# Column means of 512 of w1's columns taken later, and PSUM tiles from two halves in turn

## The chip, the cores and the metric

One core of one Trainium2 chip runs the kernel. The metric is the device time of an execution in microseconds. Engines work side by side, each through its own queue in order: TensorE (PE, with its weight loads as PEld), VectorE (DVE), ScalarE (ACT), GpSimd (POOL), and SyncE (SP), which issues DMAs.

## The reference

An input x (2048 tokens of 512 channels) goes through two layers. The first normalizes x per token, multiplies it by y, and adds x; y is a causal convolution over the 2048 tokens, per channel, of kv with ssm_k, where kv is v times a four-tap shift of k. The second normalizes the sum h per token and applies a two-layer perceptron with ReLU.

```python
x = A_q
h = x + A(layernorm(x), A_k, A_v, A_shift_k, A_ssm_k, A_ssm_D)
h2 = h + relu(layernorm(h) @ B_w1) @ B_w2        # w1 is 512 x 1376, w2 is 1376 x 512
# inside A(q, k, v, ...):
kv = (sum over t of k shifted by t, times shift_k[:, t]) * v
y  = irfft(rfft(kv, 4096) * rfft(ssm_k, 4096))[:2048] + kv * ssm_D
return q * y
```

The layernorm has no learned weights. The mean of h over the channels is taken off in w1: the mean of each column of w1 is subtracted from the column once, and h goes into the product as it is; 1/std is multiplied in at the end.

## The kernel before

The convolution is a Fourier transform written as matrix products. Forward stages (`to_rows`, `taps`, `stage1`) put the filter's half-done transform into the SBUF tile BK and that of kv into BX. The **product loop** (L501 to L517) finishes both transforms and multiplies them: 8 chunks c of 4 frequencies, in each four units of kind u (`pairs`, u0 to u3) and two of kind s (`sums`, s0 and s1; tile us). A unit has one PSUM tile: TensorE's steps K fill one half of it from BK, steps X the other from BX. Then `times` runs: ScalarE copies the K half to SBUF (L442), and VectorE multiplies the X half by it into BK or BX (L494); this product is the tile's last reader. A step of a u unit is 4 matmuls; an s unit has four such steps (K1, X1, K2, X2). The order of all steps is a string: FIRST for chunk 0, OTHER for chunks 1 to 7. A unit's tile is allocated at its first step, and in the code's order released at its "=".

Then two **inverse stages**. `inv1` (L612, tile psi) has 16 blocks b of 4 groups. A group has a matmul of 256 columns from BXs (the s units' results) and two of 128 from BK (the u units' results). The matmuls from BXs of blocks 0 and 1 run ahead (`inv1_begin`). ScalarE or VectorE copies a block into the tile ax. `inv2(q)` (L686, tile pz) makes a quarter q of the tokens from ax, and `gate(q)` (L679) multiplies it by the normalized x and adds x. Quarters 0 and 1 come first, into two PSUM tiles, psZ0 and psZ; then the perceptron (`mlp1`, `mlp2`) and the other two quarters take turns. `inv2(0)` stands between `inv1` and the gate of quarter 0.

**PSUM.** Until the end of inv1 every PSUM tile comes from `bank2` (L151): 2 x 512 fp32 numbers per partition, from a pool psF (L93) of four such slots, which is all of PSUM. When psF is closed (L731), psZ and psZ0 (L732, L733) are put in its place, psZ in the first half of PSUM and psZ0 in the second.

**The column means.** `wsum` (1376 fp32 numbers per partition) is w1 added over its four blocks of 128 rows, made by GpSimd in the product loop (`add_chunks`). After the loop `column_means` (L522) multiplies it by a matrix of 1/512 to get each column's mean on all partitions: four matmuls of FS = 344 columns into two tiles pm. The second tile is copied to SBUF by ScalarE (L626). `center(n)` (L587) subtracts the means from w1 on VectorE; all four are issued after block 0 of inv1, followed by `ec_wrap(1)` and the statistics of x's first quarter. The perceptron is the first to read w1. After inv1 two matmuls of zeros (`fill`, L647, tile psz) run on TensorE.

The order of all work is written out by hand (`manual_schedule`): each engine takes its instructions in the order of the code.

Of the kernel before, what the change touches and what calls it, by code (L numbers as in the profile page):

```python
# [9 lines left out]
ALU = mybir.AluOpType  # L10
BF16 = mybir.dt.bfloat16
F32 = mybir.dt.float32
F32R = mybir.dt.float32r
I32 = mybir.dt.int32
PSUM = bass.MemoryType.PSUM
P = 128
# [40 lines left out]
def kernel(  # L57
# [13 lines left out]
    nc = tc.nc  # L71
    _, S, D = A_q.shape
    DFF = B_w1.shape[1]
# [3 lines left out]
    DC = D // P  # L77
# [5 lines left out]
    pl = _Pools(tc)  # L83
# [6 lines left out]
    turnp = pl.push("turnp")  # L90
    early = pl.push("early", side="right")
    kp = pl.push("kp", side="right")
    psum = pl.push("psF", bufs=4, space=PSUM)  # L93

# [52 lines left out]
                             bias=(pbias if neg else nbias)[:])  # L149

    def bank2(name):  # L151
        return psum.tile([P, 2, 512], F32, tag="ps", name=name)[:]

    def fill(ps, n):

        for _ in range(n):
            nc.tensor.matmul(out=ps, lhsT=zero[:], rhs=zero[:].unsqueeze(1).to_broadcast([P, 4, P]), start=True, stop=True, skip_group_check=True)  # L157

    fill(bank2("psz")[:, 0, :], 7)

    n1i = early.tile([P, 1], I32, name="n1i")
# [15 lines left out]
    for t in (identw, ident):  # L177
        nc.gpsimd.memset(t[:], 0.0)
        nc.gpsimd.affine_select(out=t[:], in_=t[:], compare_op=ALU.not_equal, fill=1.0,
                                base=0, pattern=[[-1, P]], channel_multiplier=1)  # L180
    psw = bank2("psw")[:, 0, 0:KS * DC].rearrange("p (j r) -> p j r", j=KS)
    for j in range(KS):
        nc.tensor.matmul(out=psw[:, j, :], lhsT=wrow[:, j::KS], rhs=ident[0:DC, 0:DC], start=True, stop=True, skip_group_check=True)
    fill(bank2("psz")[:, 0, :], 17)
    nc.gpsimd.iota(r2, pattern=[[2, 32], [128, 64]], base=1, channel_multiplier=0)
    pi4 = consts.tile([P, 2], I32, name="pi4")
# [73 lines left out]
    def ec_turns(q):  # L260
        w = ecw[q]
        nc.gpsimd.iota(w[:, 1, :].rearrange("p (i a n) -> p i a n", i=4, a=4), pattern=[[1, 4], [16, 4], [64, 32]],
                       base=4 * q, channel_multiplier=0)
        for h, off in ((0, 4096 + 2048), (1, 0)):
            nc.gpsimd.tensor_scalar(out=w[:, h, :], in0=w[:, 1, :], scalar1=k1o[:], scalar2=float(off),
                                    op0=ALU.mult, op1=ALU.add)

    def ec_wrap(q):
        nc.vector.tensor_single_scalar(out=ecw[q], in_=ecw[q], scalar=8191, op=ALU.bitwise_and)

    def ec_sins(q, rs=range(DC)):
        for r in rs:
            nc.scalar.activation(out=ecore[q][:, :, :, r // 2, r % 2, :], in_=ecw[q].rearrange("p h (i x) -> p h i x", i=4),
                                 func=ACT.Sin, scale=esc[:, r:r + 1], bias=ebi[:, r:r + 1])
# [73 lines left out]
    ones = consts.tile([P, P], F32R, name="ones")  # L348
# [66 lines left out]
    BXt = bxp.tile([P, 32, 66, DC * 2], F32R, tag="X", name="BX")  # L415
# [14 lines left out]
    wsum = stf[:, 0:DFF]  # L430
# [85 lines left out]
        if c in (2, 4, 5):  # L516
            add_chunks(max(c - 3, 0))  # L517

    FS = 344
    cen = {}  # L520

    def column_means(ns):  # L522
        ps = bank2("pm")
        for b, n in enumerate(ns):
            cen[n] = ps[:, b, 0:FS]
            nc.tensor.matmul(out=cen[n], lhsT=ones[:], rhs=wsum[:, n * FS:(n + 1) * FS], start=True, stop=True)
        return ps[:, :, 0:FS]

    column_means((0, 1))
    pm23 = column_means((2, 3))  # L530
    pl.pop("skp")
    pl.pop("stp")
    pl.pop("prod")
# [5 lines left out]
    def load_x(q):  # L539
        for a, src in enumerate(_tokens(x_d, 4 * q, 4)):  # L540
            nc.sync.dma_start(out=xh[q][32 * a:32 * a + 32].rearrange("p t d -> p (t d)"), in_=src)
# [14 lines left out]
    qT = [late.tile([P, 4, DC, P], BF16, name="qT0")[:]] + [None] * 3  # L556
# [15 lines left out]
    def lift(q):  # L572
        rows_T(xT[q], xh[q])

    def ln1_stats(q):
        stats(xh[q], mv1, rstd1, q)

    def ln1_norm(q, src=None):

        src = xh[q] if src is None else src  # L580
        for i in range(4):
            t = 4 * q + i
            nc.vector.tensor_scalar(out=src[:, i, :], in0=src[:, i, :], scalar1=mv1[:, t, 0:1],
                                    scalar2=rstd1[:, t, :], op0=ALU.subtract, op1=ALU.mult)
        rows_T(qT[q], src)

    def center(n):  # L587
        fs = slice(n * FS, (n + 1) * FS)
        nc.vector.tensor_tensor(out=w1[:, :, fs], in0=w1[:, :, fs],
                                in1=cen[n].unsqueeze(1).to_broadcast([P, DC, FS]), op=ALU.subtract)  # L590

    ax1 = late.tile([P, 32, 2, P], F32R, name="ax1")
    ax = (BX[:, 1].rearrange("p n k x -> p n (k x)").rearrange("p n (m c) -> p n m c", m=2), ax1[:])
# [12 lines left out]
    def inv1_begin(b):  # L606

        blocks[b] = bank2("psi").rearrange("p b (i d a n) -> p (b i) d a n", i=2, d=2, a=2)
        for i in range(4):
            inv1_mm(b, i, (0,), sums_first=True)  # L610

    def inv1(b, eng):  # L612
        n = 4 // len(eng)
        for i0, e in zip(range(0, 4, n), eng):
            begun = b in blocks and not i0
            if not begun:
                blocks[b] = bank2("psi").rearrange("p b (i d a n) -> p (b i) d a n", i=2, d=2, a=2)
            for i in range(n):
                inv1_mm(b, i, (1, 2) if begun else (0, 1, 2), i0)
            for rho in range(2):  # L620
                copy(e, ax[rho][:, :, :, 8 * b + 2 * i0:8 * b + 2 * i0 + 2 * n],
                     blocks[b][:, 0:n].rearrange("p i d a n -> p a n (i d)")[:, rho].rearrange("p (n m) c -> p n m c", m=2))

    lift(0)
    later = qT[0].rearrange("p i r t -> p (i r t)").bitcast(F32)[:, 0:2 * FS].rearrange("p (n f) -> p n f", n=2)
    nc.scalar.copy(out=later, in_=pm23)  # L626
    cen[2], cen[3] = later[:, 0], later[:, 1]
    inv1_begin(0)
    inv1_begin(1)

# [3 lines left out]
    for b in range(16):  # L634
        inv1(b, "ADAD" if b == 15 else "AD" if b == 14 else "D" if b in (7, 9, 11, 13) else "A")
        if b == 0:
            for n in range(4):
                center(n)
            ec_wrap(1)
            ln1_stats(0)  # L640
        if b == 3:
            ln1_norm(0)
        if b in (8, 9, 10, 11):
            ec_sins(1, (b - 8,))
        if b == 11:
            load_x(1)
    fill(bank2("psz")[:, 0, :], 2)  # L647
    M = bkp.tile([P, 32768], BF16, tag="K", name="M")
    top = [0]

# [25 lines left out]
    def flat(t):  # L676
        return t.rearrange("p i r t -> p (i r t)")

    def gate(q):  # L679
        nc.vector.tensor_tensor(out=flat(qT[q]), in0=pzs[q][:].rearrange("p i r a n -> p (i r a n)"), in1=flat(qT[q]), op=ALU.mult)  # L680
        nc.vector.tensor_tensor(out=flat(xT[q]), in0=flat(qT[q]), in1=flat(xT[q]), op=ALU.add)
        hT[q] = xT[q]
        nc.sync.dma_start_transpose(out=xh[q].rearrange("p i (r c) -> p (i r) c", r=DC),
                                    in_=hT[q].rearrange("p i r t -> p (i r) t"))

    def inv2(q, pool):  # L686
        pz = pool.tile([P, 4, DC, 4, 32], F32, tag="pz", name="pz")
        pzs[q] = pz
        for j in range(16):
            i, a = j // 4, j % 4  # L690
            w = min(2, 4 - a)
            n2 = 16 * a + 4 * q + i
            for rho in range(2):
                nc.tensor.matmul(out=pz[:, i, :, a:a + w, :].rearrange("p (s r) a n -> p s r (a n)", s=2),  # L694
                                 lhsT=ax[rho][:, n2 // 2, n2 % 2, :],
                                 rhs=ecore[q][:, rho, i, :, :, 32 * a:32 * a + 32 * w],
                                 start=(rho == 0), stop=(rho == 1), skip_group_check=True)
# [30 lines left out]
            if hook is not None:  # L728
                hook(i)

    pl.pop("psF")  # L731
    psz = pl.push("psZ", space=PSUM)  # L732
    psz0 = pl.push("psZ0", space=PSUM)  # L733
    ec_turns(2)
    inv2(0, psz0)
    gate(0)
    inv2(1, psz)
    pl.pop("psZ0")
# [68 lines left out]
```

## Time and profile before

| | us |
|---|---|
| median of 3 runs | 206.26 (206.26 to 206.31) |
| profiled execution | 206.31 |
| its span, first to last instruction | 204.2 |
| TensorE busy | 195.3 (96%) |
| VectorE busy | 141.0 (69%) |
| ScalarE busy | 114.7 (56%) |
| GpSimd busy | 79.6 (39%) |

The difference of 2.1 us between the execution and its span lies around the span. The mean granted TensorE clock is 0.994 of full speed. In the timeline a row gives the start and the length in us of a group of like instructions, the engine, the line, the operation, the tiles it writes and reads (out<-in), the shape, the count, and in brackets the engine's idle time before it and what ended that. Ends of matmuls are modelled, so starts are compared.

Where the stages stand in the span: product loop 48.6 to 83.6, column means 83.6 to 84.7, inv1 84.7 to 107.9, inv2 of two quarters 108.5 to 116.2, the perceptron and the rest 116.2 to 204.2.

### The profile page before, as it was taken

The numbers are of one execution on the slowest core, as the hardware profiler recorded it, in microseconds if no ns is written. First come the engines' busy times: TensorE is split into PE (matmuls) and PEld (weight loads), VectorE is DVE, ScalarE is ACT, GpSimd is POOL, SyncE is SP. The second block draws the span as 40 slices with busy tenths as digits, with TensorE's granted clock in tenths as the row PEclk, the third lists the DMA queues.
The fourth block names the chain that finished last, engine by engine and source line by source line (L and its number), as shares of the span: only waits on it lengthen the run. The fifth ranks groups of instructions, "written<-read, shape, count | busy, mean of one in ns | idle before, by whom it ended". The sixth has DMA issues, their size and how long they took to land.

```text
span 204.2 us, 4733 instructions
## 1 busy us (share of the span) xinstructions
PE 195.3 (96%) x1929; PEld 137.2 (67%) x1929; DVE 141.0 (69%) x246; ACT 114.7 (56%) x188; POOL 79.6 (39%) x127
## 2 busy tenths in 40 slices
PE   8899999898999999999999999999999999999991
PEld 2475556887899999899998844475445844444460
DVE  4999888698799998997561967995378660360131
ACT  4987875788578877686880088205940164026300
POOL 7969999960559995212003032062002200002000
PEclk9999999999999999999999999999999999999997
DMA  6999990002600000052636999997643605110011
GB/s 178 337 178 207 176 176 3 3 5 31 248 3 0 3 3 0 22 132 55 106 87 184 207 215 196 171 174 91 91 82 76 135 19 103 32 58 17 0 51 51
DMA packets 47300, 19.94 MB, mean 98 GB/s; under 512 B 42186, under 2 KB 45744, under 8 KB 47280
## 3 DMA queue, kind: packets, MB, share of 16 engines
q1 hardware_dynamic: 43616, 16.14, 41.7%
q10 hardware_dynamic: 3664, 3.51, 6.0%
q8 instruction: 15, 0.25, 0.5%
q14 instruction: 5, 0.04, 0.1%
HBM read 7.02 MB, written 2.10 MB: 45 GB/s over the span
## 4 chain that ended last, share of the span: by engine, by line
PE 88%; DVE 7%; ACT 2%; issue 1%; DVEq 0%
PE ps1m L706 19%; PE ps2m L722 19%; PE psi L603 11%; PE us L478 9%; PE pz L694 7%; PE u L456 7%; PE ps L308 7%; PE pkv L340 5%; PE psz L157 2%; PE pst L291 1%; DVE E L343 1%; DVE BK L320 1%; DVE G L227 1%; DVE E L44 1%; DVE G L225 1%
## 5 line engine op out<-in xcount | busy, mean ns | idle before, releaser
L708 ACT ACTIVATE M<-ps1m 128x512 bf16<-128x512 f32 (+1 forms) x44 | 25.1, 595 | 49.4 <-PE ps1m L706 39.0
L722 PE MATMUL ps2m<-M 128*128 128x512 bf16 (+3 forms) x187 | 38.7, 366 | 0.0
L722 PEld LDWEIGHTS <-M 128*128 128x128 bf16 (+1 forms) x187 | 18.3, 98 | 19.9
L706 PEld LDWEIGHTS <-w 128*128 128x128 bf16 (+1 forms) x176 | 17.4, 100 | 19.9
L565 POOL TENSOR_SCALAR rstd<-mv 128x4 f32<-128x4 f32 x8 | 2.2, 277 | 70.1 <-DVE mv L563 70.1
L402 POOL TENSOR_TENSOR smc<-st 64x256 fp32r<-64x256 f32 x32 | 22.8, 732 | 12.4 <-PE us L478 11.5
L724 DVE SCALAR_TENSOR_TENSOR M<-ps2m,rstd,M 128x512 bf16<-128x512 f32 (+1 forms) x13 | 9.2, 707 | 24.8 <-PE ps2m L722 16.3
L494 DVE TENSOR_TENSOR BK<-u,ktu 128x512 fp32r<-128x512 f32 x32 | 21.2, 685 | 3.5 <-ACT ktu L442 1.9
L603 PE MATMUL psi<-inv,BK 128*128 128x128 f32 x128 | 21.1, 255 | 0.0
L442 ACT COPY ktu<-u 128x512 f32<-128x512 f32 x32 | 18.0, 592 | 5.2 <-PE u L456 4.2
L603 PE MATMUL psi<-inv,BX 128*128 128x256 f32 x64 | 20.5, 337 | 0.0
L603 PEld LDWEIGHTS psi<-inv,BK 128*128 128x128 f32 x128 | 19.7, 197 | 0.0
L706 PE MATMUL ps1m<-M,w 128*128 128x512 bf16 (+1 forms) x88 | 19.3, 379 | 0.0
L706 PE MATMUL ps1m<-xT,w 128*128 128x512 bf16 (+1 forms) x88 | 19.3, 379 | 0.0
L478 PE MATMUL us<-BK,smc 64*128 64x256 f32 x128 | 14.5, 302 | 0.6 <-ACT BX L278 0.6
L456 PE MATMUL u<-BK,st 64*128 64x256 f32 x128 | 13.6, 290 | 0.2 <-DVE BX L494 0.2
L478 PE MATMUL us<-BX,smc 64*128 64x256 f32 x128 | 13.3, 282 | 0.0
L323 ACT CAST BK<-ps 128x512 fp32r<-128x512 f32 x16 | 9.4, 586 | 6.6 <-PE ps L308 4.9
L456 PE MATMUL u<-BX,st 64*128 64x256 f32 x128 | 13.0, 281 | 0.0
L603 PEld LDWEIGHTS psi<-inv,BX 128*128 128x128 f32 x64 | 12.1, 196 | 0.3 <-DVE BK L494 0.3
L561 DVE BATCH_NORM_STATS2 st<-M 128x6 f32<-128x512 bf16 x20 | 12.3, 676 | 0.0
L494 DVE TENSOR_TENSOR BX<-us,kts 128x512 fp32r<-128x512 f32 x16 | 11.0, 686 | 0.8 <-ACT kts L442 0.5
(132 smaller groups left out, 407.2 us busy)
## 6 DMA issues: line engine op xcount, KB each, us to landing
E<-in_A_ssm_k_dram SPq DMA_DIRECT2D x1, 2048.0 KB
out_dram<-M ACTq DMA_DIRECT2D x15, 128.0 KB
w<-in_B_w_dram SPq DMA_DIRECT2D x1, 1376.0 KB
M<-in_B_w_dram ACTq DMA_DIRECT2D x1, 1280.0 KB
M<-in_A_q_dram SPq DMA_DIRECT2D x8, 128.0 KB
xh<-in_A_q_dram SPq DMA_DIRECT2D x4, 128.0 KB
xr<-in_A_q_dram SPq DMA_DIRECT2D x4, 128.0 KB
out_dram<-M ACTq DMA_DIRECT2D x2, 64.0 KB
```

The source lines that it names most:

```text
L308: nc.tensor.matmul(out=pss[rp][:, gi // 2, :, gi % 2, :], lhsT=fl[rows, 2 * g:2 * g + 2, :].rearrange("p d n -> p (d n)"), rhs=f[rows].rea ...
L402: nc.gpsimd.tensor_tensor(out=smc[pq, c % 3, i, :, 64 * dp:64 * dp + 64], in0=st[pq, ks, 64:128].bitcast(F32), in1=st[pq, ks, 0:64].bitcas ...
L442: nc.scalar.copy(out=kt[:], in_=ps)
L456: nc.tensor.matmul(out=ps[:, dp, 256 * x:256 * x + 256], lhsT=t[pq], rhs=cols((BK, BX)[x], pq, k1, i), start=not begun, stop=(i == 1), til ...
L478: mm = nc.tensor.matmul(out=ps[:, k % 2, 256 * x:256 * x + 256], lhsT=smc[pq, k // 4 % 3, i, k % 4, :], rhs=cols((BK, BX)[x], pq, k, i), s ...
L494: nc.vector.tensor_tensor(out=o, in0=ps[:, :, 256:512].rearrange("p b (g x) -> p b g x", x=8), in1=kt[:].rearrange("p b (g x) -> p b g x", ...
L561: nc.vector.bn_stats(out=st[:, i, :], in_=src[:, i, :])
L603: nc.tensor.matmul(out=o if part == 0 else o[:, P * part - P:P * part], lhsT=src[:, g // 2, :, g % 2::2].rearrange("p c r -> p (c r)"), rh ...
L694: nc.tensor.matmul(out=pz[:, i, :, a:a + w, :].rearrange("p (s r) a n -> p s r (a n)", s=2), lhsT=ax[rho][:, n2 // 2, n2 % 2, :], rhs=ecor ...
L706: nc.tensor.matmul(out=ps1[:fsz, :].rearrange("p (i t) -> p i t", i=4), lhsT=w1[:, c, fc * P:fc * P + fsz], rhs=hT[sc][:, :, c, :], start= ...
L708: nc.scalar.activation(out=h1T[:fsz, fc, :], in_=ps1[:fsz, :], func=ACT.Relu)
L722: nc.tensor.matmul(out=ps2, lhsT=h1T[:ksz, fc, i * P:(i + 1) * P], rhs=w2[:ksz, fc, d0:d0 + w], start=(fc == 0), stop=(fc == NFC - 1))
```

## The change

The pool of four slots becomes two pools of two slots, psFa and psFb; `bank2` takes from them in turn. The columns of w1 are cut into 512, 352 and 512. The means of the first two parts are taken where all were before, into one tile. The sums of the last part are copied by ScalarE to an unused piece of the tile BX (`wlast`); their means are taken after inv1, in place of one of the two matmuls of zeros, in a tile of the first half. The copy of the second pm tile to SBUF is gone. The first two parts are centered after block 0 of inv1 as before, the last between `inv2(0)` and `gate(0)`.

```diff
-    psum = pl.push("psF", bufs=4, space=PSUM)
+    psum = [pl.push(n, bufs=2, space=PSUM) for n in ("psFa", "psFb")]
+    turn = [0]
...
     def bank2(name):
-        return psum.tile([P, 2, 512], F32, tag="ps", name=name)[:]
+        turn[0] += 1
+        return psum[turn[0] % 2].tile([P, 2, 512], F32, tag="ps", name=name)[:]
...
-    FS = 344
+    THIRDS = ((0, 512), (512, 864), (864, DFF))
     cen = {}
-    def column_means(ns):
-        ps = bank2("pm")
-        for b, n in enumerate(ns):
-            cen[n] = ps[:, b, 0:FS]
-            nc.tensor.matmul(out=cen[n], lhsT=ones[:], rhs=wsum[:, n * FS:(n + 1) * FS], start=True, stop=True)
-        return ps[:, :, 0:FS]
-
-    column_means((0, 1))
-    pm23 = column_means((2, 3))
+    def column_means(ps, n, sums):
+        cen[n] = ps[:, 0:THIRDS[n][1] - THIRDS[n][0]]
+        nc.tensor.matmul(out=cen[n] if n < 2 else cen[n].rearrange("p (g x) -> p g x", x=16), lhsT=ones[:], rhs=sums, start=True, stop=True)
+
+    pm = bank2("pm")
+    for n in range(2):
+        column_means(pm[:, n], n, wsum[:, slice(*THIRDS[n])])
+    wlast = BXt[:, :, 32:34, :].rearrange("p g k x -> p g (k x)")
+    nc.scalar.copy(out=wlast, in_=wsum[:, slice(*THIRDS[2])].bitcast(F32).rearrange("p (g x) -> p g x", x=16))
...
     def center(n):
-        fs = slice(n * FS, (n + 1) * FS)
+        fs = slice(*THIRDS[n])
         nc.vector.tensor_tensor(out=w1[:, :, fs], in0=w1[:, :, fs],
-                                in1=cen[n].unsqueeze(1).to_broadcast([P, DC, FS]), op=ALU.subtract)
+                                in1=cen[n].unsqueeze(1).to_broadcast([P, DC, fs.stop - fs.start]), op=ALU.subtract)
...
     lift(0)
-    later = qT[0].rearrange("p i r t -> p (i r t)").bitcast(F32)[:, 0:2 * FS].rearrange("p (n f) -> p n f", n=2)
-    nc.scalar.copy(out=later, in_=pm23)
-    cen[2], cen[3] = later[:, 0], later[:, 1]
     inv1_begin(0)
...
         if b == 0:
-            for n in range(4):
+            for n in range(2):
                 center(n)
...
-    fill(bank2("psz")[:, 0, :], 2)
+    turn[0] = 1
+    pm2 = bank2("pm2")
+    column_means(pm2[:, 0], 2, wlast)
+    fill(pm2[:, 1], 1)
...
-    pl.pop("psF")
+    pl.pop("psFb")
+    pl.pop("psFa")
     psz = pl.push("psZ", space=PSUM)
     psz0 = pl.push("psZ0", space=PSUM)
     ec_turns(2)
     inv2(0, psz0)
+    center(2)
     gate(0)
```

## The prediction

> **What bounds the kernel now.** I read the page's chain first, then the waits of TensorE, then the timelines of TensorE and VectorE around the tiles that the change renames, and last the windows with the granted clock (1.00 in each that I asked for). The chain is TensorE nearly throughout:
>
> ```profile
> PE 88%; DVE 7%; ACT 2%; issue 1%; DVEq 0%
> PE ps1m L706 19%; PE ps2m L722 19%; PE psi L603 11%; PE us L478 9%; PE pz L694 7%; PE u L456 7%; PE ps L308 7%; PE pkv L340 5%; PE psz L157 2%; PE pst L291 1%; DVE E L343 1%; DVE BK L320 1%; DVE G L227 1%; DVE E L44 1%; DVE G L225 1%
> ```
>
> From the first psi matmul (84.66) on, the chain has one break of 0.64 us, the last copies before pz; so what TensorE loses up to psi arrives at the end. The product loop (u, us) looks full, but starts of steps show small waits for PSUM. TensorE, eighth chunk:
>
> ```profile
> 79.35 0.51 PE L478 MATMUL us<-BK,smc 64*128 64x256 f32 x4
> ...
> 80.93 0.41 PE L478 MATMUL us<-BX,smc 64*128 64x256 f32 x4
> ...
> 82.47 0.40 PE L456 MATMUL u<-BK,st 64*128 64x256 f32 x4
> 82.71 0.41 PE L456 MATMUL u<-BX,st 64*128 64x256 f32 x4
> 82.95 0.41 PE L456 MATMUL u<-BK,st 64*128 64x256 f32 x4
> 83.19 0.41 PE L456 MATMUL u<-BX,st 64*128 64x256 f32 x4
> 83.55 1.08 PE L526 MATMUL pm<-st,ones 128*128 128x344 f32 x4
> ```
>
> The steps shown are s0K1, s0X2, u3K, u3X, u2K, u2X, and the column means. A step is 4 matmuls in two pairs and takes 0.24 us, 0.12 a pair. VectorE, whose product is the last reader of a unit's tile, in the order u0, s0, u1, s1, then u3 and u2, then the centering:
>
> ```profile
> 81.26 0.69 DVE L494 TENSOR_TENSOR BK<-u,ktu 128x512 fp32r<-128x512 f32 x1 [0.27 <-ACT ktu L442]
> 81.99 0.69 DVE L494 TENSOR_TENSOR BX<-us,kts 128x512 fp32r<-128x512 f32 x1
> 82.72 0.69 DVE L494 TENSOR_TENSOR BK<-u,ktu 128x512 fp32r<-128x512 f32 x1
> 83.33 0.68 DVE L494 TENSOR_TENSOR BX<-us,kts 128x512 fp32r<-128x512 f32 x1
> 83.92 1.28 DVE L494 TENSOR_TENSOR BK<-u,ktu 128x512 fp32r<-128x512 f32 x2
> ```
>
> **Which tile gets which slot** decides this case. u3K starts at 82.47, while the product of s0 runs until 82.68: so u3 doesn't stand in s0's slot but in u0's, read out at 81.96. s0K1 starts 0.15 after the previous chunk's product of u1 ends (79.20), u0K 0.11 after s1's (79.80). One rule fits all of them: a tile takes the free slot that was released first in program order, of four. A second fit: the third psi block starts at 87.68, before the second centering from pm ends (88.19), so it has the slot that the ScalarE copy left free, not pm's.
>
> **The change, part by part.** *Two halves (added to every tile).* Tiles now alternate between two pools of two. Up to the product loop each tile still takes the slot of the tile four before it: nothing. In the loop 54 tiles have gone before; from the second chunk the six units are allocated s0, u0, u1, s1, u3, u2, so s0, u1 and u3 share one half, u0, s1 and u2 the other. When u3 comes, its half holds s0 and u1. It must wait for s0's product, in each of seven chunks; the free slot in the other half is of no use to it. The first chunk has another order, in which u3 gets u0's slot as now.
>
> The price of one wait: in the second chunk s0's product ends at 57.37 and u3K started at 57.15; the same form of wait is in the trace at the first chunk's u3, which starts 0.05 after u0's product (52.06), and its step takes 0.35 instead of 0.24:
>
> ```profile
> 52.11 0.51 PE L456 MATMUL u<-BK,st 64*128 64x256 f32 x4
> 52.46 0.41 PE L478 MATMUL us<-BK,smc 64*128 64x256 f32 x4
> ```
>
> So u3K comes at 57.42, 0.27 late, and what follows is 0.38 late. Part is given back: before s0K1 stood a wait of 0.13 (s0K1 at 58.24) and this goes; s0K1 of the third chunk starts 57.42 + 0.11 + 8 pairs of 0.12 = 58.48, 0.24 late. From there on each chunk has this period: s0K1 to the last pair of s0X2, 13 pairs or 1.55; from it (81.05 by the timeline) to the end of s0's product (82.69), 1.64; the wait 0.05; u3K's extra 0.11; 8 pairs 0.96. Sum 4.30. Now it is (79.35 - 58.24) / 5 = 4.22. Five periods add 5 x 0.08 = 0.40, and s0K1 of the eighth chunk is 0.64 late. Bounds for the growth of a chunk: 0, if the spare time takes it up, and 0.18, if u1K stops too: by the same reckoning its slot comes free 0.16 ahead of it, and u0K, with 0.11 ahead in the rows, loses 0.05, s0K1, which waits, 0.09; a full 0.10 is the end. I take 0.08, the sum of the rows.
>
> In the eighth chunk the two short losses after s0K1 and u0K (0.09 and 0.05) no longer stand ahead of s0X2, so s0's product is 0.64 - 0.14 = 0.50 late (83.19), u3K at 83.24, u3X and u2 0.88 late. u3's ScalarE copy moves from 83.16 to 84.04 and takes 0.59, its product starts at 84.66, u2's 0.60 behind, and ends at 85.94 instead of 85.20: **0.74 late**.
>
> *Column means: four matmuls of 344 columns become two of 512 and 352.* The four take 83.55 to 84.66, but mostly wait: the third starts 0.05 after s1's product (84.00), the first psi 0.05 after u3's (84.60), the fifth (85.25) 0.05 after u2's. With one pm tile fewer, psi blocks 0 to 2 get the slots of s1, u3 and u2. The second pass (L603 on BK) needs u2's product anyway and starts 0.05 behind it. That frees 85.84 - 85.25 = 0.59 against now. It isn't the bound, though:
>
> *Centering, 2048 and 1408 elements instead of 4 x 1376, and who waits for it.* The fourth psi block now takes pm's slot, since its half holds pm and block 1 only, and pm is released by the second centering. The rows:
>
> ```profile
> 85.12 3.07 DVE L589 TENSOR_TENSOR w<-w,pm 128x1376 bf16<-128x1376 bf16 x2
> ...
> 89.10 0.34 PE L603 MATMUL psi<-inv,BX 128*128 128x256 f32 x1
> ```
>
> Two of 1376 take 3.07, the second starting 1.49 behind the first; 2048 then cost 2.19 until the next starts, and 1408 end 1.61 later: 3.80. They begin when u2's product is nearly through: 85.86 to 89.66. The fourth block starts at 89.72 instead of 89.10, 0.62 late, and loses 0.10 after the wait as above: **0.72**. Behind the centering on VectorE stand the sine wrap and the statistics of the first quarter; they come 1.5 us earlier, with the transpose on SP's queue behind them, and the gate reads its result 12 us later: nothing.
>
> *ScalarE's copy* of 688 columns (0.74) becomes one of 512 (0.59 by a copy of that size), ahead of the wait for u2's product, where ScalarE idles 1.07 us: nothing; uncovered it would cost 0.59. SP's load of x waits for u2's product as now. *The last 512 columns* run in the place of one of two fill matmuls (107.71 to 108.31) while TensorE waits for copies until 108.54: nothing; uncovered, 0.39. *center(2)* is queued on VectorE ahead of the gate, and TensorE's second inv2 needs pm2's slot:
>
> ```profile
> 112.54 2.29 DVE L680 TENSOR_TENSOR qT<-pz,qT 128x2048 bf16<-128x2048 f32 x1 [4.15 <-PE pz L694]
> ```
>
> By this row of the same size it takes 2.29, from 108.43 to 110.72; the second inv2 starts at 112.28. Covered by 1.56 us; uncovered, 2.29.
>
> **Sum.** 0.72 us on the profiled execution, span 204.2 and 206.31 in all, 0.05 above the median of 206.26: **207.0**. With a growth of 0 and 0.18 a chunk, 0.72 - 0.40 and 0.72 + 0.50: 206.6 to 207.5, its own range.
>
> **Rivals.** *The waits add up in full.* All seven cost 0.38 and nothing is given back: 2.66, 208.9. For it: TensorE is full in the loop's windows (4.20 of 4.20). Against: the 0.13 and 0.14 that the starts show as spare. Chance 0.10. *Nothing measurable.* The slots fall otherwise than I read, or the loop's wait is absorbed; then the fourth psi block starts at 85.12 + 3.80 + 0.05 = 88.97, with 0.10 lost: 206.3. For it: u3's wait is only 0.22 beyond now. Chance 0.16. *Faster.* The early psi blocks, no longer behind the last product, carry it: the loop's wait stays in the loop's spare time, the fourth block finds its slot read out in time, and the 0.59 freed ahead of the second pass stays, less 0.10 after the wait: 205.8. It decides only if centering ends before 88.6, 0.4 sooner than the rows say, or pm's slot isn't the one taken. Chance 0.10. *The clock drops.* With more short stops, TensorE's granted clock falls in the loop; one chunk at half speed is 32 pairs of 0.12, 3.8 us: 210. Against: 1.00 in the first chunk too, where TensorE stands 0.57 of 4.30. Chance 0.02. The Trainium skill (TensorE: Matmul & The Clock Gate, A second HAM failure mode: psum-queue depth-cycling) says that short stops from cycling through PSUM can throttle the clock on and off; by that rule this rival holds, and the trace so far doesn't agree.
>
> **How the numbers follow.** 0.62 for the forecast. A run can tell 0.2% from no change, 0.41 us, so slower is above 206.67: nearly all of the forecast, with the first and the last rival, 0.71; faster, below 205.85, is most of the third, 0.08; within, 0.21. The range takes in the forecast, no change, and part of the first rival: 206.2 to 208.2.
>
> **What would show it.** Right: from the second chunk u3K starts 0.05 behind s0's product and the chunks measure 4.30; s0K1 no longer 0.15 behind u1's; u2's product near 85.9; the fourth psi block 0.05 behind the second centering; all behind it later by one amount. Wrong: u3K before the end of s0's product, chunks still of 4.22, a psi stage that starts earlier, or a second inv2 that waits for center(2).

## The result and the profile after

The changed kernel takes 207.34 us (median of 6 runs, 207.23 to 207.76) beside 206.28 for the kernel before on the same chip; the ratio is 1.0052, with a 95% interval of 1.0039 to 1.0065. It is slower by 1.06 us. The profiled execution took 207.26, 0.95 more than the one before; its span is 205.08, so 2.18 lie around the span (2.14 before), and 0.91 of the loss is within the span. The chain of work that ended last:

```profile
PE 84%; DVE 9%; ACT 3%; issue 2%; DVEq 0%
PE ps1m L711 19%; PE ps2m L727 19%; PE psi L608 9%; PE u L459 7%; PE pz L699 7%; PE us L481 7%; PE ps L311 7%; PE pkv L343 5%; PE psz L160 2%; PE pst L294 1%; DVE E L346 1%; DVE BK L497 1%; DVE BK L323 1%; DVE w L594 1%; DVE BX L497 1%
```

TensorE has given 4% of the chain to others, among them the products (L497) and the centering (L594, w). The timeline of the last chunk of the product loop, TensorE first (the rows shown are s0K1, s1X2, u3K and u3X):

```profile
80.18 0.41 PE L481 MATMUL us<-BK,smc 64*128 64x256 f32 x4
...
83.03 0.41 PE L481 MATMUL us<-BX,smc 64*128 64x256 f32 x4
83.46 0.51 PE L459 MATMUL u<-BK,st 64*128 64x256 f32 x4
83.81 0.41 PE L459 MATMUL u<-BX,st 64*128 64x256 f32 x4
```

and VectorE, the products of u0, s0, u1, s1, u3 and u2 and then the centering:

```profile
81.98 0.69 DVE L497 TENSOR_TENSOR BK<-u,ktu 128x512 fp32r<-128x512 f32 x1 [0.17 <-ACT ktu L445]
82.71 0.69 DVE L497 TENSOR_TENSOR BX<-us,kts 128x512 fp32r<-128x512 f32 x1
83.53 0.69 DVE L497 TENSOR_TENSOR BK<-u,ktu 128x512 fp32r<-128x512 f32 x1
84.14 0.68 DVE L497 TENSOR_TENSOR BX<-us,kts 128x512 fp32r<-128x512 f32 x1
84.87 1.29 DVE L497 TENSOR_TENSOR BK<-u,ktu 128x512 fp32r<-128x512 f32 x2
86.08 3.81 DVE L594 TENSOR_TENSOR w<-w,pm 128x2048 bf16<-128x2048 bf16 x2
```

From s1X2 to u3K it takes 0.43 us instead of 0.25 (82.22 to 82.47 before): u3K starts 0.06 behind the end of s0's product (83.40). A waiting TensorE hardly shows as idle time here, since the modelled ends of its matmuls cover the wait; it is read from the starts. The step that waited is longer too: from u3K to u3X is 0.35 (83.46 to 83.81) instead of 0.24. This is so in each chunk from the second to the eighth. Busy time over one chunk (columns: length of the window, then for PE, PEld, DVE, ACT and POOL busy us and instructions, the granted clock, and the DMA's share and GB/s):

```profile
71.49:75.84 4.35, 4.33 (x69) 4.06 (x66) 3.95 (x7) 3.41 (x7) 4.21 (x4) 1.00 0.00 0
```

The chunks measure 4.35, and before 4.22, at full clock. Behind the loop, the starts of the last group of the third psi block and the first of the fourth:

```profile
89.22 0.34 PE L608 MATMUL psi<-inv,BX 128*128 128x256 f32 x1
90.03 0.36 PE L608 MATMUL psi<-inv,BX 128*128 128x256 f32 x1 [0.29 <-DVE w L594]
```

A group takes 0.36; the fourth block comes 0.81 behind, and 0.15 after the second centering's end (89.89). Before, it started at 89.10. So it is 0.93 late, and pz, at 109.46 instead of 108.54, is 0.92 late: inverse stage and perceptron hand on the delay that they get. The late centering is hidden:

```profile
109.33 2.29 DVE L594 TENSOR_TENSOR w<-w,pm 128x2048 bf16<-128x2048 bf16 x1
```

It ends at 111.62, the second inv2 starts at 113.20, and VectorE idles 1.84 us before the gate at 113.46.

### The profile page after: what moved, and what is told of

The parts are those of the page before. It is cut to its first block, busy times and chain, and to the rows that moved or that the text cites. A ratio compares the mean times of both kernels' runs of the same rounds, so it can differ in the third digit from the quotient of the medians.

```text
span 205.1 us, 4731 instructions
## 1 busy us (share of the span) xinstructions
PE 196.7 (96%) x1927; PEld 137.5 (67%) x1927; DVE 141.9 (69%) x245; ACT 115.2 (56%) x188; POOL 79.4 (39%) x127
## 4 chain that ended last, share of the span: by engine, by line
PE 84%; DVE 9%; ACT 3%; issue 2%; DVEq 0%
PE ps1m L711 19%; PE ps2m L727 19%; PE psi L608 9%; PE u L459 7%; PE pz L699 7%; PE us L481 7%; PE ps L311 7%; PE pkv L343 5%; PE psz L160 2%; PE pst L294 1%; DVE E L346 1%; DVE BK L497 1%; DVE BK L323 1%; DVE w L594 1%; DVE BX L497 1%
## 5 line engine op out<-in xcount | busy, mean ns | idle before, releaser
L497 DVE TENSOR_TENSOR BK<-u,ktu 128x512 fp32r<-128x512 f32 x32 | 21.3, 688 | 3.8 <-PE us L481 1.3
L497 DVE TENSOR_TENSOR BX<-us,kts 128x512 fp32r<-128x512 f32 x16 | 11.0, 687 | 0.8 <-ACT kts L445 0.5
```

The lines of the kernel that those rows point to most:

```text
L497: nc.vector.tensor_tensor(out=o, in0=ps[:, :, 256:512].rearrange("p b (g x) -> p b g x", x=8), in1=kt[:].rearrange("p b (g x) -> p b g x", ...
```

## The experiments

The theory has two waits, that of u3 in the loop and that of the fourth psi block for the centering. Four kernels follow: one takes both waits away, two take one each, and one puts the halves alone into the kernel before. The kernel before took 206.39 beside them.

**Both waits away: two tiles at a time from each half.**

```diff
         turn[0] += 1
-        return psum[turn[0] % 2].tile(...)
+        return psum[(turn[0] + 1) // 2 % 2].tile(...)
...
-    turn[0] = 1
```

> The changed kernel, but the two halves are taken two tiles at a time. Each unit of the product loop then has the slot it had with four slots in one row (u3 that of u0), and the fourth psi block that of the first block instead of pm's. Theory (both waits, u3 for s0's product and the fourth psi block for the second centering, make the loss): chunks of 4.22 us again, the second psi pass 0.05 behind u2's product, no wait for centering, so the 0.59 us freed ahead of it stay less about 0.1: 205.8, faster than before. Rival (the moved column means or their copy cost the time, the halves nothing): 207.3, as the changed kernel.

205.78 us, ratio 0.9968 (0.9953 to 0.9982): faster than both kernels. The rows are s0's product and u3K in the last chunk, then the second centering, the last group of the third psi block and the first of the fourth:

```profile
82.12 0.69 DVE L497 TENSOR_TENSOR BX<-us,kts 128x512 fp32r<-128x512 f32 x1
82.60 0.40 PE L459 MATMUL u<-BK,st 64*128 64x256 f32 x4
```

```profile
87.45 1.61 DVE L594 TENSOR_TENSOR w<-w,pm 128x1408 bf16<-128x1408 bf16 x1
...
88.40 0.34 PE L608 MATMUL psi<-inv,BX 128*128 128x256 f32 x1
...
88.75 0.34 PE L608 MATMUL psi<-inv,BX 128*128 128x256 f32 x1
```

u3K again starts before s0's product ends (82.81), chunks are 4.21, and the fourth block starts at 88.75, 0.35 behind the group ahead of it and before the centering ends (89.06). The rival falls: with the moved means and the ScalarE copy as in the change, the loss is gone.

**Only the loop's wait away.**

```diff
-        return psum[turn[0] % 2].tile(...)
+        return psum[((turn[0] + 1) // 2 if turn[0] <= 102 else turn[0] + 1) % 2].tile(...)
...
-    turn[0] = 1
+    turn[0] = 124
```

> The changed kernel with halves two tiles at a time in the product loop alone; from pm on one at a time, so that the fourth psi block still has pm's slot. Theory: u2's product ends at 85.2 again, the two centerings at 88.93, the fourth psi block starts near 89.05 where before it started at 89.10: 206.3, as before. Rival (the loop's waits are most of it by themselves, and nothing waits for centering): 205.8. Rival (the loop's waits cost nothing): 207.3.

206.01, ratio 0.9983 (0.9960 to 1.0007), between the theory's 206.3 and the first rival's 205.8. The trace decides; the centerings and the fourth block's first matmul:

```profile
85.44 3.81 DVE L594 TENSOR_TENSOR w<-w,pm 128x2048 bf16<-128x2048 bf16 x2
```

```profile
89.39 0.36 PE L608 MATMUL psi<-inv,BX 128*128 128x256 f32 x1
```

The second centering ends at 89.25 and the block starts 0.14 behind, so it does wait. Where most of the missing 0.3 us comes from is told with the last copies below.

**Only the fourth block's wait away.**

```diff
+        if b == 2:
+            turn[0] += 1
```

> The changed kernel with one turn left out before the fourth psi block, which so gets the first block's slot in the other half, not pm's; the product loop is unchanged with its seven waits. Theory: u2's product stays at 86.16, the fourth psi block starts at 89.58 instead of 90.03, 0.45 sooner: 206.9. Rival (nothing waits for centering, the loop's delay alone is what arrives): 207.3.

206.70, ratio 1.0021 (1.0003 to 1.0040). Its profiled execution (208.55) lost some 2 us early, at a granted clock of 0.66 between 10 and 15 us, so it is read from the loop's end on: u2's product ends at 88.24, and the fourth block starts 3.42 later, where the changed kernel needs 3.87. That is the 0.45 expected; the loop's part of the loss stays.

**The halves alone, in the kernel before.**

```diff
-    psum = pl.push("psF", bufs=4, space=PSUM)
+    psum = [pl.push(n, bufs=2, space=PSUM) for n in ("psFa", "psFb")]
...
-        return psum.tile(...)
+        turn[0] += 1
+        return psum[turn[0] % 2].tile(...)
```

> The kernel before with its slots split into two halves in turn and nothing else changed; all column means stay where they were. Theory: the loop's seven waits appear, u2's product ends at 86.16, 0.96 late; the third psi block takes the first block's slot and waits some 0.3 to 0.45 for its copies: 207.2 to 207.7, slower. Rival (the halves are harmless, the moved means are the loss): 206.3.

207.81, ratio 1.0068 (1.0050 to 1.0086): slower, with no column mean moved, with chunks of 4.34, and a little above the 207.2 to 207.7 expected. The third psi block waits, though not for the copies that I named but for the second centering, which ends 0.15 ahead of it, at 89.74:

```profile
89.89 0.36 PE L605 MATMUL psi<-inv,BX 128*128 128x256 f32 x1 [0.50 <-DVE w L591]
```

So the rule that the slot released first in the code's order comes first isn't the whole rule: the first block's last copy stands ahead of the centering in the code. Here the half gave pm's slot first; in the run with pairs, where centering is longer, it gave the first block's. How the slots are ordered when two releases lie close together stays open; in the product loop and for the fourth block of the change no such choice arises.

**One pool of four instead of halves.** This run asks what the halves are for. The kernel before took 206.29 beside this run and the next, and 206.34 beside the three after them.

```diff
-    psum = [pl.push(n, bufs=2, space=PSUM) for n in ("psFa", "psFb")]
+    psum = pl.push("psF", bufs=4, space=PSUM)
...
-    turn[0] = 1
```

> The changed kernel with one pool of four slots in place of the halves; the column means are moved as in the change. Theory: loop and early psi blocks as in the kernel before, 0.5 gained; but in the row of four the late tile of means falls on a slot in that half of PSUM which the first inv2 takes, so the first inv2 waits for the last centering, some 2.2 us: 208.0. Rival (that wait is hidden or doesn't arise): 205.8.

208.97, ratio 1.0120 (1.0087 to 1.0154). The median stands between two groups: two executions took 208.22 and 208.32, near the 208.0 expected, and two took 209.63 and 209.64, one of them the profiled one. The mean granted clock is 0.996 in the first two and 0.991 in the others. The profiled one shows where the clock went: the first matmul of inv2, and the stretches of time around and behind it (columns as above; the granted clock is the third number from the end):

```profile
110.35 0.36 PE L696 MATMUL pz<-core,BX 128*128 128x256 f32 x1 [2.47 <-DVE w L592]
```

```profile
110.00:112.00 2.00, 1.65 (x13) 1.68 (x14) 0.21 (x1) 0.00 (x0) 0.00 (x0) 0.93 1.07 360
112.00:114.00 2.00, 2.00 (x11) 2.00 (x11) 0.00 (x0) 0.00 (x0) 0.00 (x0) 0.50 1.34 284
```

TensorE stood 2.47 us for the last centering, as expected, and 1.4 us after work resumed the clock fell to half: the first inv2 took 5.30 (110.35 to 115.65) instead of 3.74. In this execution the stop cost itself and 1.56 more.

**One pool, late means one slot on.**

```diff
-    turn[0] = 1
+    fill(bank2("psz")[:, 0, :], 1)
     pm2 = bank2("pm2")
     column_means(pm2[:, 0], 2, wlast)
-    fill(pm2[:, 1], 1)
```

> As the run with one pool of four slots, but the matmul of zeros has a tile of its own ahead of the late tile of means, which so falls on the next slot, in the half that the second inv2 takes. Theory: the centering is hidden again behind the first inv2, and the gain ahead of the second psi pass stays: 205.8, without any halves. Rival (the late means or their centering cost time wherever their slot is): 206.3 or more.

A miss: 209.76, ratio 1.0133 (1.0099 to 1.0167), in executions of 208.11 to 211.35, of which the longest is the profiled one. The first inv2 waited again: centering ended at 110.67, it started at 110.81, and the clock fell. Either my count of slots was wrong, or the slot doesn't matter. Two more runs put the late means, by the same count, on the two slots that were left:

```diff
+    for _ in range(2):      # 3 in the other run
+        nc.tensor.matmul(out=bank2("psz")[:, 0, 0:P], lhsT=zero[:], rhs=zero[:], start=True, stop=True, skip_group_check=True)
     pm2 = bank2("pm2")
```

> One pool of four slots, with two small tiles of zeros ahead of the late tile of means, which so moves on to the next slot of the four. Theory (a popped pool passes on all its slots together): the first inv2 waits for the last centering wherever the late means lie, as in both runs with one pool: it starts 0.14 behind the centering's end, 2.2 us late. Rival (only the slot under the first inv2's own half holds it up): in some of the four positions the first inv2 starts 0.15 behind the last copy of the inverse stage.

> The same with three small tiles ahead, the last of the four positions. Theory: again the first inv2 starts 0.14 behind the last centering. Rival: here or with two small tiles it starts behind the last copy, and the time is near 205.8.

208.64 and 210.00, of one execution each. With two spare tiles centering ended at 110.80 and the first inv2 started at 110.86; with three, at 110.58 and 110.63. The wait in the last:

```profile
PE pz L698 <- DVE w L592: 2.4, 1, 2.4
```

With none, one, two or three tiles ahead of the late means, the first inv2 waits for the last reader of the closed pool. If the count is right, these are all four slots, and a closed pool's slots are passed on together; the traces show the waits, not the slots. In the change the second pool spares the first inv2 this wait: it starts at 109.46, and the last centering ends at 111.62. With two spare tiles the clock stayed at 1.00, with three it fell to 0.50; the stops were 2.4 us in both.

**The last copies of the inverse stage.** Two of the runs came out 0.2 to 0.3 faster than expected (206.01 for 206.3, 206.70 for 206.9). In these, and in the run with both waits away, the first inv2 starts 0.75 or 0.76 behind the last psi matmul; in the change and before it is 0.96. What the three share is that the last piece of psi lies in the half of the second inv2.

```diff
+        if b == 4:
+            turn[0] += 1
```

> The changed kernel with one turn left out before the sixth psi block: loop and centering wait as in the change, but the last piece of the inverse stage has its tile in the half that the second inv2 takes, not the first. Theory: the first inv2 then waits for the first of VectorE's two last copies only, not also for the second, and starts 0.76 instead of 0.96 behind the last psi matmul: 207.1. Rival (that wait is for the data, not for the slot): 207.3.

207.30, the rival's time and not the 207.1 expected; the ratio is 1.0036 (1.0023 to 1.0048), beside 1.0052 (1.0039 to 1.0065) for the change. The intervals overlap, so the time alone doesn't decide. The trace does (the last two copies and the first inv2 matmul):

```profile
109.25 0.29 DVE L283 CAST BX<-psi 128x128 fp32r<-128x128 f32 x1 [0.28 <-PE psi L608]
...
109.45 0.28 DVE L283 CAST ax<-psi 128x128 fp32r<-128x128 f32 x1
109.69 0.36 PE L701 MATMUL pz<-core,BX 128*128 128x256 f32 x1
```

inv2 starts 0.15 behind the first copy, which has its data, before the second ends at 109.73. In the change it starts 0.15 behind the second (109.31), whose result its first matmul doesn't read.

The profiled execution of this run reached the loop's second chunk 0.41 later than that of the change, which hides the gain in its time. Counted from that chunk's first step to the first inv2, the traces have 54.87 us before, 55.82 in the change and 55.64 here: 0.18 less than the change. By the same count both waits away give 54.16, the loop's alone 54.61 and the fourth block's alone 55.15. Against before that is 0.71 and 0.26 less and 0.28 more. The theory with 0.2 for the last copies gives 0.7 and 0.25 less and 0.3 more.

## Why the prediction held

The time, 207.34 for 207.0, is in the forecast's own range, and the mechanism is the one predicted, in both of its places. The loss was put too small: 0.72 forecast, 0.92 at the first inv2 in the trace, 1.06 between the medians. The runs don't say where the last 0.1 between trace and medians comes from.

*u3 waits for s0's product.* Right in each of seven chunks, 0.055 behind each time. The third chunk's s0K1 was put at 58.48 and came at 58.46. The waits of 0.15 before s0K1 are gone, as predicted: u1's product is done 0.3 ahead of it.

*The period of a chunk* was the mis-sized term: 4.30 predicted, (80.18 - 58.46) / 5 = 4.345 measured. Of its parts, s0K1 to the last pair of s0X2 takes 1.58 for 1.55, the others (1.64, 0.055, and 1.07 from u3K to the next s0K1) are as told. The terms of the prediction add up to 4.31, which it gave as 4.30. Over five chunks the difference makes 0.22, and u2's product ends at 86.16 for 85.94: 0.96 late, not 0.74.

*Centering and the fourth block.* The two centerings take 3.81 for a predicted 3.80, and the block waits for them. It starts 0.93 late, not 0.62: 0.22 more comes from the loop, and 0.10 more from starting 0.15 and not 0.05 behind the centering. In return the loss after the wait is 0.03, not 0.10. The run without this wait (3.42 for 3.87) shows its size.

*What was put at nothing*: ScalarE's copy (0.62 at 85.22, the next work at 87.41), the late means, and center(2) with 1.58 to spare for a predicted 1.56. None of it delays what follows.

*The rivals.* Full price in every chunk (208.9): no, the s0K1 wait was given back. Nothing measurable: no. Faster at 205.8: not in this kernel, but with the waits away it is what came, 205.78. Of that gain the traces put 0.2 on the last copies, which that expectation didn't have, so its hit to 0.02 is partly luck. The clock: 1.00 in every chunk, though TensorE stops in each from the second on (in the last chunk the pair ahead of u3K starts at 83.16 and u3K at 83.46, 0.30 apart instead of 0.12). The rule of the Trainium skill (TensorE: Matmul & The Clock Gate, A second HAM failure mode: psum-queue depth-cycling) isn't borne out by such stops of 0.2 us every 4.35 us.

The rule for slots, which the prediction rested on, was right for u3 and the fourth block and failed in the run with halves alone. The prediction didn't see the 0.2 of the last copy; it is in the kernel before too, so the change neither brings nor removes it.

## What to carry to other kernels

A split of a pool into halves keeps its number of slots but not which tile gets which: write down, for the order in which tiles are allocated and released, whose slot each gets, and compare it with the time at which that slot's last reader is done. Where releases don't come in the order of allocation, halves in strict turn can send a tile to a slot still in use while one in the other half is free; two from each half at a time took the waits away here, and the kernel then gained from the moved work. A late reader of a pool that is about to be replaced is better kept in a pool of its own: here the replacement waited for it in all four runs with one pool.

## What the runs showed of the hardware

A single stop of TensorE of 2.4 to 2.5 us could halve the granted clock. In the profiled executions with one pool it fell to 0.50 in three of four: for 3.4 us from 1.4 us after work resumed (no spare tile, 1.56 us lost in the first inv2), for 3.4 us from 1.2 us after (three), and for 6.8 us from 0.8 us before work resumed (one, whose first inv2 took 6.50 instead of 3.74). With two spare tiles, whose stop was as long, it stayed at 1.00. The Trainium skill (TensorE: Matmul & The Clock Gate, Part 1: The HAM clock gate) has the clock fall to half after an idle window of about 3.4 us; the half clock agrees, but here less idle time was enough, and not each time. Stops of 0.2 us in each chunk of the loop left it at 1.00.

After a wait in the product loop the next pair of matmuls came 0.22 to 0.23 behind instead of 0.12, so there a wait cost TensorE about 0.1 more than its length; at the fourth psi block it was 0.03.
